# Scores in two column tiles of 256 rows in a cached-attention decode kernel, with another row order for the K load

## Chip, cores, metric

One core of one Trainium2 chip runs the whole program. The metric is the device time of one execution in microseconds (us). Every ratio is to runs of the kernel before on the same chip. Where kernels from different chips are set side by side (eight with eight_apart, four_apart with the changed kernel), the kernel before took 1147.5 to 1152.7 us on each of them. Each run has a state: slow when it is over 1.5% above the fastest run of the same kernel, otherwise fast.

## The reference, cut to what matters

Four blocks run one after the other: attention over a cache (A), a mixer with an MLP (B), A again, B again. One token for each of 8 batch elements, so nearly all of the work is reading the cache, twice.

```python
# A: B=8, Sq=1, D=448, Hq=16, Hkv=8, Sk=4096, Dh=256, bf16
q = (x @ wq).reshape(B, Sq, Hq, Dh).transpose(0, 2, 1, 3)
k = jnp.repeat(k_cache, 2, axis=1);  v = jnp.repeat(v_cache, 2, axis=1)
p = softmax(einsum("bhqd,bhkd->bhqk", q, k) * Dh ** -0.5)
o = einsum("bhqk,bhkd->bhqd", p, v)
...
x = x + A(layernorm(x));  x = x + B(layernorm(x))
x = x + A(layernorm(x));  x = x + B(layernorm(x))
```

K and V together have 268 MB, or 256 loads of 1 MB for one pass. Of the 512 loads of two passes the kernel makes 424; the other 88 tiles stay on the chip from the first pass to the second.

## The kernel before

A task is one batch element with two K/V heads: 8192 rows of K and as many of V, loaded in four K tiles and four V tiles of 1 MB, each 128 partitions by 8 KB. Fifteen such slots hold loads in flight. For each K tile, VectorE turns 32x32 blocks in place, TensorE multiplies with the block-diagonal query, and when all four tiles of a task are done, ScalarE takes exp and TensorE turns p, so that P times V can follow.

```python
# loads: 128 rows of 8 KB for a tile, all on the SP queue
if kv:
    src = rows.rearrange("(a p y) d -> a p (y d)", a=4, y=16)[c]
else:
    src = rows.rearrange("(p x y) d -> x p (y d)", x=4, y=16)[c]
nc.sync.dma_start(dst[:], src)
...
def scores(sc, t, x, qbd, gp):        # 4 column tiles (k) of 128 columns
    kv = t[:].rearrange("p (k t e i r) -> p k e r t i", k=4, t=4, e=4, r=2)
    for n in range(8):
        ...
        for k in range(4):
            nc.tensor.matmul(sc[32 * k : 32 * k + 8, 128 * x : 128 * x + 128],
                             qbd[:, ep, gp].rearrange("p a h -> p (a h)"),
                             kv[:, k, 2 * half + e2, par], start=(n == 0), stop=(n == 7))
...
ptw = consts.tile([128, 4, 16, 14], BF16, name="ptw")   # p with 6 zeros on each side
```

In these access patterns the first dimension counts partitions on the chip's side. On the memory's side of the K load it counts p = 0 to 127, each 64 rows of the cache (32 KB) after the last: one pitch, one count of 128.

Of the kernel before, what the change touches and what calls it, by code (L numbers as in the profile page):

```python
# [17 lines left out]
def kernel(  # L18
# [77 lines left out]
    for u in range(2):  # L96
        nc.vector.tensor_reduce(
            usel[:, 2 * u : 2 * u + 2],
            ident.rearrange("p (k q h) -> p h k q", k=4, h=2)[:, :, :, 2 * u : 2 * u + 2],
            mybir.AxisListType.XY,  # L100
            ALU.add,
        )
# [6 lines left out]
        ALU.add,  # L109
    )  # L110

    ptw = consts.tile([128, 4, 16, 14], BF16, name="ptw")
    nc.vector.memset(ptw[:], 0.0)

    misc = ps_t.tile([128, 512], FP32, name="misc")
    ot_bank = misc[:, 256:384]
# [252 lines left out]
    def z_cols(zall, gps):  # L369

        np_ = len(gps)
        zm = chn.tile([128, 4, np_], FP32, tag=f"zm{np_}")
        nc.vector.tensor_tensor(
            zm[:],
            zall[:, gps[0] : gps[-1] + 1].unsqueeze(1).to_broadcast([128, 4, np_]),
            usel[:].unsqueeze(2).to_broadcast([128, 4, np_]),
            ALU.mult,
        )
        yield
        z_ps = misc[:, 480 : 480 + 4 * np_].rearrange("p (n g) -> p n g", n=4)  # L380
        nc.tensor.matmul(z_ps, ones, zm[:], start=True, stop=True)  # L381
        yield
        rz = chn.tile([128, 4, np_], FP32, tag=f"rz{np_}")
        nc.vector.reciprocal(rz[:], z_ps)  # L384
        return rz
# [9 lines left out]
    def half(o_ps, zall, g8, OT):  # L395


        rz = yield from z_cols(zall, range(2 * g8, 2 * g8 + 2))

        R = chn.tile([128, 8], FP32, tag="R")  # L400
        nc.vector.tensor_mul(
            R[:].rearrange("p (g n) -> p g n", n=4),
            rz[:].rearrange("p n g -> p g n"),
            fold[:].rearrange("p (g n) -> p g n", n=4),
        )
        o_sb = chn.tile([128, Dh], FP32, tag="o_sb")
        nc.scalar.copy(o_sb[:], o_ps[:, Dh * g8 : Dh * g8 + Dh])
        yield
        ot_ps = ot_bank[:, 64 * g8 : 64 * g8 + 16].rearrange("p (j h) -> p j h", j=2)
        for j in range(2):  # L410
            nc.tensor.matmul(  # L411
                ot_ps[:, j], o_sb[:, 128 * j : 128 * j + 128], R[:], start=True, stop=True
            )
        yield
        nc.vector.tensor_copy(OT[:, :, 8 * g8 : 8 * g8 + 8], ot_ps)
        yield

# [15 lines left out]
    def first_half(b, st):  # L433

        OT = work.tile([128, 2, Hq, 1], BF16, tag="OT", bufs=1)
        y_ps = ps_m.tile([128, 4, 1], FP32, tag="chain")
        st["OT"], st["y"] = OT, y_ps
        yield from half(st["o"], st["z"], 0, OT[:, :, :, 0])
        yield from add_half(y_ps, OT, 0, 1, True, 2)
# [82 lines left out]
    def emit_loads(most=None):  # L522
        n = 0
        while loads and places and n != most:
            it = loads.pop(0)
            p = where[it] = places.pop(0)
            if stays(it):
                where[tasks[it[0]][1:], it[1:]] = p
            t, kv, c = it
            _, b, gp = tasks[t]  # L530
            dst = slots[p]
            rows = (A_v_cache if kv else A_k_cache)[b, 2 * gp : 2 * gp + 2].rearrange(
                "g s d -> (g s) d"
            )
            if kv:
                src = rows.rearrange("(a p y) d -> a p (y d)", a=4, y=16)[c]
            else:
                src = rows.rearrange("(p x y) d -> x p (y d)", x=4, y=16)[c]
            nc.sync.dma_start(dst[:], src)  # L539
            n += 1  # L540

# [5 lines left out]
            nc.vector.transpose(w, w)  # L547

    def scores(sc, t, x, qbd, gp):
        kv = t[:].rearrange("p (k t e i r) -> p k e r t i", k=4, t=4, e=4, r=2)  # L550
        for n in range(8):
            half, e2, par = n // 4, (n // 2) % 2, n % 2
            ep = 4 * e2 + 2 * par + half
            for k in range(4):
                nc.tensor.matmul(  # L555
                    sc[32 * k : 32 * k + 8, 128 * x : 128 * x + 128],
                    qbd[:, ep, gp].rearrange("p a h -> p (a h)"),
                    kv[:, k, 2 * half + e2, par],
                    start=(n == 0),
                    stop=(n == 7),  # L560
                )

    def exps(p_sb, sc, zall, gp):
        nc.scalar.activation(  # L564
            p_sb[:].rearrange("p t i x -> p x t i"),
            sc[:].rearrange("p (x t i) -> p x t i", x=4, t=4),
            ACT.Exp,
            scale=scale_exp,
            accum_out=zall[:, gp : gp + 1],
        )  # L570

    def transpose_p(p_sb):

        pt_ps = misc[:, 0:128].rearrange("p (t k r) -> p t k r", t=4, k=4)
        cols = identb[:].rearrange("p (k r) -> p k r", k=4)[:, :, 0:8]
        for t in range(4):
            nc.tensor.matmul(  # L577
                pt_ps[:, t],
                p_sb[:, t].rearrange("p i x -> p (i x)"),
                cols,  # L580
                start=True,
                stop=True,
            )
        nc.scalar.copy(  # L584
            ptw[:, :, :, 6:8],
            pt_ps.rearrange("p t k (a h) -> p a (t k) h", a=4),
        )

    def pv(o_ps, v, a, gp, begin):


        g = 2 * gp + a // 2
        w = 6 - 2 * (g % 4)
        for y in range(16):
            q = y % 4
            nc.tensor.matmul(  # L596
                o_ps[32 * q : 32 * q + 8, 256 * (g // 4) : 256 * (g // 4) + 256],
                ptw[:, a, 4 * (y % 4) + y // 4, w : w + 8],
                v[:, y * Dh : (y + 1) * Dh],
                start=(begin and y < 4),  # L600
                stop=(y >= 12),
                skip_group_check=True,
            )

    def pv_cols(o_ps, v, a, gp):

        g = 2 * gp + a // 2
        for y in range(16):
            for j in range(2):
                nc.tensor.matmul(  # L610
                    o_ps[:, j, 2 * g : 2 * g + 2],
                    v[:, y * Dh + 128 * j : y * Dh + 128 * j + 128],
                    ptw[:, a, 4 * (y % 4) + y // 4, 6:8],
                    start=(a % 2 == 0 and y == 0 and j == 0),
                    stop=(a % 2 == 1 and y == 15),
                    skip_group_check=True,
                )
# [24 lines left out]
    def add_gen(kind, b, g, at, until, total):  # L642
        gens.append({"kind": kind, "b": b, "g": g, "at": at, "until": until, "n": 0, "of": total})
# [20 lines left out]
    for idx, it in enumerate(items):  # L664
# [5 lines left out]
        if kv == 0:  # L670
# [9 lines left out]
                run(spread_q(st["qT"][:] if ps == 1 else qT1[:, :, b], qbd))  # L680
                st["q"] = qbd
            if "o" not in st:
                z_t = chn.tile([128, GP], FP32, tag="zall", bufs=3)
                st["o"], st["z"] = o_banks[0], z_t
                o_banks.append(o_banks.pop(0))
                if final:
                    st["y"] = o_banks[0][:, 0:4].unsqueeze(2)
                    oc = st["o"][:, 0 : 2 * Hq].rearrange("p (j h) -> p j h", j=2)
            if not (ps == 1 and stays(it)):
                transpose_k(slot)  # L690
            step(idx)
            scores(sc_t[n % 2], slot, c, st["q"], gp)
            if c == 0 and n > 0:
                transpose_p(p_of.pop(n - 1))
            if c == 3:
                p_n = work.tile([128, 4, 32, 4], BF16, tag="p_sb", bufs=1)
                p_of[n] = p_n
                exps(p_n, sc_t[n % 2], st["z"], gp)
        else:
            st = state[ps, b]  # L700
            if n in p_of:
                transpose_p(p_of.pop(n))
            if final and gp in free and c == 1:
                rz_gp = run(z_cols(st["z"], [gp]))
            step(idx)
# [22 lines left out]
            if c == 3:  # L728
                done = pairs_done[ps, b] = pairs_done.get((ps, b), 0) + 1
                if done == 2 and ps == 0:  # L730
                    add_gen("chain", b, first_half(b, st), idx + 1, idx + 21, 9)
                elif done == 2:
                    add_gen("chain" if final else "last", b, first_last(b, st), idx + 1, idx + 13, 9)
                elif done == 4 and ps == 0:
                    add_gen("chain", b, chain(b, st), idx + 1, first_of[(1, b), 0] - 1, 30)
                elif done == 4 and not final:
                    add_gen("last", b, last(b, st), idx + 1, idx + (7 if b == Bn - 2 else 13), 6)
                    if b == Bn - 2:
                        add_gen("last", 0, rest(b, st), idx + 1, len(items) - 2, 21)
        if not (ps == 0 and stays(it)):  # L740
# [83 lines left out]
```

## Time and profile before

| | before |
|---|---|
| median of 3 runs | 1147.85 us (1147.19 to 1150.88) |
| load queue's share of the 16 DMA engines' span | 98.0% |
| mean rate | 398 GB/s |
| TensorE, VectorE, ScalarE busy | 61%, 48%, 10% |
| chain of waits, K loads | 62% |

The page of the kernel before. Its row of GB/s has one number for each fortieth of the span; then come the packet counts, the queues (packets, MB, share of 16 engines' time), the chain that ended last, and four groups of instructions (count; busy us, mean ns of one; idle time before them and what ended most of it):

```profile
GB/s 352 375 420 420 407 385 399 418 412 383 414 420 400 385 399 419 420 403 406 409 420 420 400 400 413 420 420 387 402 412 420 408 371 412 420 410 355 410 420 153
DMA packets 68349, 457.52 MB, mean 398 GB/s; under 512 B 6999, under 2 KB 13030, under 8 KB 13542
## 3 DMA queue, kind: packets, MB, share of 16 engines
q1 hardware_dynamic: 68198, 455.19, 98.0%
...
## 4 chain that ended last, share of the span: by engine, by line
DMA 69%; PE 13%; DVE 11%; SPq 3%; issue 2%; POOL 1%; ACT 0%; POOLq 0%; DVEq 0%; ACTq 0%
DMA slot<-in_A_k_cache_dram 62%; DVE slot L547 9%; DMA slot<-in_A_v_cache_dram 6%; PE sc L555 4%; PE o L596 3%; PE y_ps L318 2%; SPq L148 2%; PE q_ps L274 1%; DMA wq_sb<-in_A_wq_dram 1%; SPq L539 1%; PE o L610 1%; DVE qbd L300 1%; PE o L318 1%; PE h_ps L336 0%; PE misc L381 0%
```

```profile
L547 DVE STREAM_TRANSPOSE slot<-slot 128x1024 uint32<-128x1024 uint32 x400 | 472.7, 1222 | 383.7 <-DMA slot<-in_A_k_cache_dram 375.0
L555 PE MATMUL sc<-slot,qbd 128*8 128x128 bf16 x8192 | 280.6, 286 | 345.6 <-DVE slot L547 287.2
...
L596 PE MATMUL o<-slot,ptw 128*8 128x256 bf16 x3968 | 242.8, 388 | 55.8 <-DMA slot<-in_A_v_cache_dram 33.9
L564 ACT ACTIVATE p_n<-sc 128x512 bf16<-128x512 f32 x64 | 84.7, 1323 | 780.6 <-PE sc L555 780.6
```

The loads fill the queue: 98.0% of what 16 engines have, and plateaus of 420 GB/s. 455 MB at 420 GB/s would be 1084 us, so the time is the DMA's but for some 65 us. "Under 512 B 6999": 6996 of these small packets have 4 bytes, and their count fits one completion packet for every DMA engine that took part in a load.

Stretches of the kernel before (columns: window in us; length; busy us of each engine with instruction counts; granted TensorE clock; DMA share; GB/s):

```profile
880.00:890.00 10.00, 4.27 (x96) 2.48 (x95) 4.51 (x5) 1.32 (x2) 0.00 (x0) 0.50 1.01 420
890.00:900.00 10.00, 4.48 (x100) 2.65 (x100) 4.74 (x4) 0.27 (x1) 0.00 (x0) 0.50 1.02 424
...
920.00:930.00 10.00, 7.82 (x177) 5.99 (x174) 6.68 (x17) 0.00 (x0) 0.70 (x1) 0.50 0.94 336
```

In the first two stretches, at 420 and 424 GB/s, TensorE is busy less than half of the time. Where a chain of small projections runs (920 to 930 us), TensorE nears 8 of 10 us and the load rate drops to 336. A busy TensorE alone does not lower the rate: between 1080 and 1090 us it was busy for 9.05 of 10 us, at 420 GB/s.

The timeline before, two score halves of one K tile, the P times V that follows, and the issue of a V load (start, us, engine, line; in brackets idle time before and what ended it):

```profile
885.92 0.60 PE L555 MATMUL sc<-slot,qbd 128*8 128x128 bf16 x16 [2.38 <-DVE slot L547]
...
887.04 0.60 PE L555 MATMUL sc<-slot,qbd 128*8 128x128 bf16 x16 [0.53 <-DVE slot L547]
...
887.82 1.02 PE L596 MATMUL o<-slot,ptw 128*8 128x256 bf16 x16 [0.18 <-DMA slot<-in_A_v_cache_dram]
...
888.89 0.33 SPq L539 DMA_DIRECT2D slot<-in_A_v_cache_dram  x1
```

Sixteen matmuls of 128 columns, four column tiles at a time, take 0.60 us; sixteen of 256 columns, four at a time, take 1.02 us.

### The profile page before, as it was taken

To read this page: it belongs to the slowest core of one execution; us is meant where nothing else is said; L and a number is where in the kernel's file an instruction comes from. 1 tells how busy PE (TensorE), PEld (TensorE's weight loads), DVE (VectorE), ACT (ScalarE), POOL (GpSimd) and SP (SyncE) were. 2 spreads that over 40 slices of the span, in tenths; PEclk is the share of its full clock that TensorE was granted. 3 is DMA by queue.
4 is the path that set the end of the run, shared out by engine and by line. 5 is a ranking of instruction groups with operands and counts; after the bars stand their busy time and mean duration, and the time that the engine had idled before them with its cause. 6 is when DMAs were issued, how large, how long until landed. Compare 5 with 4: busy or idle time off the path is not lost.

```text
span 1149.6 us, 36707 instructions
## 1 busy us (share of the span) xinstructions
PE 705.3 (61%) x17177; PEld 514.0 (45%) x17177; DVE 548.2 (48%) x904; ACT 113.9 (10%) x234; POOL 15.6 (1%) x25
## 2 busy tenths in 40 slices
PE   3144677457755667456764676646665576647787
PEld 2023455345533455344542454425443365425666
DVE  5145453455354544546254553445534553445352
ACT  0001011100110011001110101010011001100100
POOL 0000000000000000000000000000000000000000
PEclk9999997655655556555565557555575556555655
DMA  9999999999999999999999999999999999999993
GB/s 352 375 420 420 407 385 399 418 412 383 414 420 400 385 399 419 420 403 406 409 420 420 400 400 413 420 420 387 402 412 420 408 371 412 420 410 355 410 420 153
DMA packets 68349, 457.52 MB, mean 398 GB/s; under 512 B 6999, under 2 KB 13030, under 8 KB 13542
## 3 DMA queue, kind: packets, MB, share of 16 engines
q1 hardware_dynamic: 68198, 455.19, 98.0%
q8 instruction: 134, 2.20, 0.8%
q14 instruction: 17, 0.14, 0.0%
HBM read 455.15 MB, written 0.01 MB: 396 GB/s over the span
## 4 chain that ended last, share of the span: by engine, by line
DMA 69%; PE 13%; DVE 11%; SPq 3%; issue 2%; POOL 1%; ACT 0%; POOLq 0%; DVEq 0%; ACTq 0%
DMA slot<-in_A_k_cache_dram 62%; DVE slot L547 9%; DMA slot<-in_A_v_cache_dram 6%; PE sc L555 4%; PE o L596 3%; PE y_ps L318 2%; SPq L148 2%; PE q_ps L274 1%; DMA wq_sb<-in_A_wq_dram 1%; SPq L539 1%; PE o L610 1%; DVE qbd L300 1%; PE o L318 1%; PE h_ps L336 0%; PE misc L381 0%
## 5 line engine op out<-in xcount | busy, mean ns | idle before, releaser
L547 DVE STREAM_TRANSPOSE slot<-slot 128x1024 uint32<-128x1024 uint32 x400 | 472.7, 1222 | 383.7 <-DMA slot<-in_A_k_cache_dram 375.0
L555 PE MATMUL sc<-slot,qbd 128*8 128x128 bf16 x8192 | 280.6, 286 | 345.6 <-DVE slot L547 287.2
L555 PEld LDWEIGHTS <-qbd 128*8 128x8 bf16 x8192 | 194.5, 105 | 430.8 <-issue 298.6
L596 PE MATMUL o<-slot,ptw 128*8 128x256 bf16 x3968 | 242.8, 388 | 55.8 <-DMA slot<-in_A_v_cache_dram 33.9
L564 ACT ACTIVATE p_n<-sc 128x512 bf16<-128x512 f32 x64 | 84.7, 1323 | 780.6 <-PE sc L555 780.6
L596 PEld LDWEIGHTS <-ptw 128*8 128x8 bf16 x3968 | 107.9, 109 | 93.8 <-issue 45.0
L318 PEld LDWEIGHTS <-wo_sb 128*128 128x128 bf16 (+1 forms) x1600 | 64.8, 124 | 16.2 <-issue 15.6
L318 PE MATMUL y_ps<-OT,wo_sb 128*128 128x1 bf16 (+1 forms) x1280 | 55.5, 177 | 1.5 <-issue 1.5
L384 DVE RECIPROCAL rz<-misc 128x8 f32<-128x8 f32 (+1 forms) x33 | 6.4, 193 | 96.3 <-PE misc L381 96.3
L274 PEld LDWEIGHTS <-wq_sb 128*128 128x128 bf16 x1152 | 33.9, 104 | 19.1 <-issue 17.3
L274 PE MATMUL q_ps<-xb,wq_sb 128*128 128x1 bf16 (+1 forms) x1152 | 35.3, 166 | 11.4 <-DMA wq_sb<-in_A_wq_dram 3.6
L584 ACT CAST ptw<-misc 128x128 bf16<-128x128 f32 x64 | 17.5, 274 | 211.9 <-PE misc L577 159.4
L411 PEld LDWEIGHTS misc<-R,o_sb 128*128 128x128 f32 x124 | 25.9, 293 | 11.0 <-issue 11.0
L318 PEld LDWEIGHTS <-w_sb 128*128 128x128 bf16 (+1 forms) x630 | 25.7, 125 | 7.3 <-issue 5.2
L411 PE MATMUL misc<-R,o_sb 128*128 128x8 f32 x124 | 28.8, 343 | 0.0
L232 POOL TENSOR_TENSOR t<-t,nhalf 128x2 f32<-128x2 f32 (+1 forms) x17 | 10.7, 630 | 1075.8 <-DVE t L239 978.0
L318 PE MATMUL y_ps<-HT_t,w_sb 128*128 128x1 bf16 (+1 forms) x560 | 24.2, 177 | 0.5 <-DVE HT_t L359 0.5
L300 DVE TENSOR_SCALAR qbd<-misc,quad 128x64 bf16<-128x64 f32 x64 | 13.8, 278 | 22.0 <-PE misc L294 22.0
L381 PE MATMUL misc<-zm,one 128*128 128x8 f32 (+1 forms) x66 | 18.1, 348 | 6.7 <-ACT ptw L584 6.7
L336 PEld LDWEIGHTS <-w_sb 128*128 128x128 bf16 x560 | 17.2, 105 | 9.6 <-issue 9.2
L336 PE MATMUL h_ps<-xb,w_sb 128*128 128x1 bf16 (+1 forms) x560 | 17.9, 166 | 4.9 <-DVE xb L249 4.6
L381 PEld LDWEIGHTS misc<-zm,one 128*128 128x128 f32 x66 | 15.2, 287 | 11.9 <-ACT ptw L584 8.4
(92 smaller groups left out, 207.7 us busy)
## 6 DMA issues: line engine op xcount, KB each, us to landing
slot<-in_A_v_cache_dram SPq DMA_DIRECT2D x224, 1024.0 KB, 12.3
slot<-in_A_k_cache_dram SPq DMA_DIRECT2D x200, 1024.0 KB, 16.4
wo_sb<-in_A_wo_dram SPq DMA_DIRECT2D x1, 3584.0 KB, 26.6
wq_sb<-in_A_wq_dram SPq DMA_DIRECT2D x3, 1024.0 KB, 7.0
w_sb<-in_B_w_dram SPq DMA_DIRECT2D x1, 1568.0 KB, 12.8
w_sb<-in_B_w_dram SPq DMA_DIRECT2D x3, 448.0 KB, 26.8
wq_sb<-in_A_wq_dram SPq DMA_DIRECT2D x2, 256.0 KB, 10.0
w_sb<-in_B_w_dram SPq DMA_DIRECT2D x2, 112.0 KB, 9.0
```

The costliest lines, as they stand in the source:

```text
L148: nc.sync.dma_start(t[:, fc * cols : (fc + 1) * cols], src[fc * 128 : fc * 128 + 128, :])
L274: nc.tensor.matmul(q_ps[:, j * Hq + h, :], w, xbs(nb)[:, xi, :], start=(fc == 0), stop=(fc == 3),)
L300: nc.vector.tensor_scalar_mul(qbd[:, :, :, a, :], qs.rearrange("p e (f g u h) -> p (e f) u g h", f=2, u=2, h=2)[:, :, u], quad[:, a : a + 1],)
L318: nc.tensor.matmul(r, w[:, i, lo:hi], rhs(i), start=(first and fc == 0 and i == rows[0]), stop=(stop and i == rows[-1]), skip_group_check= ...
L336: nc.tensor.matmul(h_ps[:, c * nb : c * nb + nb], w, xbs(nb)[:, xi, :], start=(fc == 0), stop=(fc == 3),)
L381: nc.tensor.matmul(z_ps, ones, zm[:], start=True, stop=True)
L411: nc.tensor.matmul(ot_ps[:, j], o_sb[:, 128 * j : 128 * j + 128], R[:], start=True, stop=True)
L547: nc.vector.transpose(w, w)
L555: nc.tensor.matmul(sc[32 * k : 32 * k + 8, 128 * x : 128 * x + 128], qbd[:, ep, gp].rearrange("p a h -> p (a h)"), kv[:, k, 2 * half + e2, ...
L564: nc.scalar.activation(p_sb[:].rearrange("p t i x -> p x t i"), sc[:].rearrange("p (x t i) -> p x t i", x=4, t=4), ACT.Exp, scale=scale_ex ...
L584: nc.scalar.copy(ptw[:, :, :, 6:8], pt_ps.rearrange("p t k (a h) -> p a (t k) h", a=4),)
L596: nc.tensor.matmul(o_ps[32 * q : 32 * q + 8, 256 * (g // 4) : 256 * (g // 4) + 256], ptw[:, a, 4 * (y % 4) + y // 4, w : w + 8], v[:, y * ...
```

## The change

The intent is fewer instructions on TensorE (4096 score matmuls of 256 columns in place of 8192 of 128), exp and turning of p after every second K tile, and a smaller buffer for p in which neighbours share their zeros. Two column tiles of 256 rows need each half task to hold 1024 consecutive rows of each of the four blocks of 2048, so the K load's row order changes too.

```diff
-                src = rows.rearrange("(p x y) d -> x p (y d)", x=4, y=16)[c]
+                src = rows.rearrange("(a u i x y) d -> u x a i (y d)", a=4, u=2, x=2, y=16)[c // 2, c % 2]
             nc.sync.dma_start(dst[:], src)
 ...
-        kv = t[:].rearrange("p (k t e i r) -> p k e r t i", k=4, t=4, e=4, r=2)
+        kv = t[:].rearrange("p (k t e i r) -> p k e r t i", k=2, t=8, e=4, r=2)
 ...
-            for k in range(4):
+            for k in range(2):
                 nc.tensor.matmul(
-                    sc[32 * k : 32 * k + 8, 128 * x : 128 * x + 128],
+                    sc[32 * k : 32 * k + 8, 256 * (x % 2) : 256 * (x % 2) + 256],
 ...
-            sc[:].rearrange("p (x t i) -> p x t i", x=4, t=4),
+            sc[:].rearrange("p (x t i) -> p x t i", x=2, t=8),
 ...
-    def transpose_p(p_sb):
-        pt_ps = misc[:, 0:128].rearrange("p (t k r) -> p t k r", t=4, k=4)
-        for t in range(4):
+    def transpose_p(p_sb, u):
+        pt_ps = misc[:, 0:128].rearrange("p (t k r) -> p t k r", t=8, k=2)
+        for t in range(8):
             nc.tensor.matmul(
-                pt_ps[:, t],
+                pt_ps[64 * u : 64 * u + 64, t],
 ...
-    ptw = consts.tile([128, 4, 16, 14], BF16, name="ptw")
+    ptw = consts.tile([128, 6 + 8 * 64], BF16, name="ptw")
 ...
+            if c == 2:
+                transpose_p(p_of.pop(n), 0)
-            if c == 3:
-                p_n = work.tile([128, 4, 32, 4], BF16, tag="p_sb", bufs=1)
+            if c % 2 == 1:
+                p_n = work.tile([128, 8, 32, 2], BF16, tag="p_sb", bufs=1)
```

Left out: the sum of exp kept by half task and added once, the addressing of the smaller buffer for p, the copy of o in two halves of 128 columns, and step counts of the interleaved chains.

## The prediction

> **What bounds the kernel now.** The DMA engines. The page gives the load queue 98% of the 16 engines' span, at 398 GB/s mean; the stretches view shows 419 to 424 GB/s between 850 and 910 us, with TensorE under 70% busy. 455 MB at 420 GB/s is 1084 of the 1149.6 us. The chain of waits is 62% waits for K loads. Each K load (200) and V load (224) is 1 MB in 128 rows of 8 KB; one packet of 8 KB takes 309 ns (26.5 GB/s for an engine).
>
> **What the change does on the engines.** Scores go from 8192 matmuls of 128 columns, four column tiles side by side, to 4096 of 256 columns, two side by side. The timeline shows 0.60 us for half of a K load's scores; P times V, with 16 matmuls of 256 columns four side by side, takes 1.03 us. Eight of 256 columns two side by side stream as long, so I expect 1.0 us a half: 0.8 us more of TensorE for each K load (estimate). Exp goes from 64 of 1.32 us to 128 of half the size (estimate 0.75 us), turning from 4 to 8 matmuls a task. With two loads taking 5 us, most of that hides; alone it would cost 0 to 4%, in stretches where the queue already drops to 336 to 390 GB/s.
>
> **The decisive part: the K load.** To put 256 rows in two tiles, its source becomes four blocks (1 MB apart) of 32 rows: the outermost count of the source is 4 where it was 128. The Trainium skill, "DMA: Bandwidth & Descriptors", section "Why a DMA increments its semaphore by 16 and not by 1", says that the engines used are the largest number up to 16 that divides the outermost counts of both sides: 4 here. This trace agrees for other shapes: it has 6996 four-byte completion packets; 436 loads x 16, plus 8, 7 and 4 for the transfers with outer counts 8, 7 and 4, make 6995. So four engines carry all of K: 200 x 1.05 MB / 4 = 52.4 MB each, plus a sixteenth of the rest, 15.3 MB: 67.8 MB at 26.5 GB/s = 2560 us, plus about 40 us of ends, all on the critical path.
>
> **A second cost.** Each of the four engines then writes 32 neighbouring partitions. By the skill's "SBUF — State Buffer", section "Door 1: The DMA port swizzle", partitions p and p+32 share a port, so engines 0 and 1 collide when in step, as do 2 and 3. In this trace the 64-row loads, where engines pair up on ports, show 4 KB packets from 156 to over 315 ns: half rate. Fully in step, a K load would take 19.8 instead of 9.9 us, the kernel some 4500 us. [...] I expect about 400 us of it.
>
> **Prediction: 3000 us, range 2550 to 4100.** Faster by over 2%: 3%; within 2%: 5%; slower: 92%.
>
> **What would show it.** Per K load 4 landings instead of 16; mean rate near 150 GB/s; DMA share near 0.4; K issue to landing over 60 us against 16.4; DVE's wait for K over five times 375 us; the chain over 85% K loads. K packets of 309 ns would show no port sharing, 600 ns full sharing.
>
> **What would make it wrong.** If the load still spreads over 16 engines, 1150 to 1200 us, set by the longer scores. If the ports don't collide, 2600 us; if engines stay in step, 4500 us.

## The result

| | before | after |
|---|---|---|
| median | 1147.52 us (4 runs) | 3113.0 us (3077.47 to 3125.63, 4 runs) |
| ratio | | 2.7009, 95% interval 2.6764 to 2.7254 |
| load queue's share | 98.0% | 50.0% |
| mean rate | 398 GB/s | 149 GB/s |

Ratios are the mean time of one kernel's fast runs over that of the other's of the same rounds, so they are not quite the ratio of the medians. One of the four runs after, that of 3125.63 us, counts as slow; the three fast ones took 3077.47, 3105.6 and 3120.4 us. The sums below use the median of all four, 3113.0.

The page of the kernel after, the same lines:

```profile
GB/s 156 181 140 143 145 156 144 153 142 164 148 144 144 149 167 155 138 144 143 170 152 145 143 148 163 139 140 139 136 159 137 143 140 162 136 150 144 167 147 130
DMA packets 65924, 457.10 MB, mean 149 GB/s; under 512 B 4599, under 2 KB 10630, under 8 KB 11142
## 3 DMA queue, kind: packets, MB, share of 16 engines
q1 hardware_dynamic: 65798, 455.18, 50.0%
...
## 4 chain that ended last, share of the span: by engine, by line
DMA 81%; SPq 7%; DVE 5%; PE 5%; another core or an unknown queue 1%; issue 1%; ACT 0%; POOLq 0%; DVEq 0%
DMA slot<-in_A_k_cache_dram 77%; SPq L546 5%; DVE slot L554 5%; DMA slot<-in_A_v_cache_dram 4%; PE sc L562 3%; SPq L151 1%; PE o L604 1%; SPq L635 0%; PE misc L584 0%; DVE qbd L303 0%; PE o L321 0%; PE o L618 0%; PE q_ps L277 0%; PE h_ps L339 0%
```

```profile
L562 PE MATMUL sc<-slot,qbd 128*8 128x256 bf16 x4096 | 482.3, 386 | 2038.2 <-DVE slot L554 2008.5
L554 DVE STREAM_TRANSPOSE slot<-slot 128x1024 uint32<-128x1024 uint32 x400 | 474.3, 1224 | 2286.2 <-DMA slot<-in_A_k_cache_dram 2286.2
...
L604 PE MATMUL o<-slot,ptw 128*8 128x256 bf16 x3968 | 275.3, 382 | 39.1 <-DMA slot<-in_A_v_cache_dram 28.0
L571 ACT ACTIVATE p_n<-sc 128x512 bf16<-128x512 f32 x128 | 95.4, 746 | 2095.1 <-PE sc L562 2067.8
```

The same 455 MB move at 149 GB/s. The small packets fell from 6999 to 4599: 2400 fewer, which is 200 K loads times 12. So 4 engines finish each K load where 16 did. VectorE's idle time before the turning of K went from 384 to 2286 us, nearly all of it waiting for a K load. The chain of waits is 77% K loads. The new score matmuls and exps are not where the time went: TensorE is busy for 963 of 3076 us.

Stretches of the kernel after, 2 us each:

```profile
1519.00:1521.00 2.00, 1.51 (x32) 0.93 (x26) 0.00 (x0) 0.27 (x1) 0.00 (x0) 1.00 0.25 102
1521.00:1523.00 2.00, 0.00 (x0) 0.00 (x0) 0.00 (x0) 0.00 (x0) 0.00 (x0) 0.81 0.25 107
1523.00:1525.00 2.00, 0.00 (x0) 0.08 (x1) 1.11 (x1) 0.00 (x0) 0.00 (x0) 0.50 0.63 172
1525.00:1527.00 2.00, 1.70 (x22) 0.92 (x23) 1.26 (x2) 0.00 (x0) 0.00 (x0) 0.50 1.04 279
1527.00:1529.00 2.00, 1.72 (x20) 0.95 (x14) 0.00 (x0) 0.79 (x2) 0.00 (x0) 0.50 0.73 176
1529.00:1531.00 2.00, 0.00 (x0) 0.00 (x0) 0.00 (x0) 0.00 (x0) 0.00 (x0) 0.50 0.22 82
1531.00:1533.00 2.00, 0.00 (x0) 0.00 (x0) 0.00 (x0) 0.00 (x0) 0.00 (x0) 0.50 0.26 111
```

Two regimes can be seen. At 102 to 111 GB/s and a DMA share of 0.25, four of 16 engines work and each moves some 26 GB/s: K alone. Between 1523 and 1529 us a V load passes on all 16 engines, and the rate is 172 to 279 GB/s, where the kernel before had 420. The share of 1.04 there is not full speed, since before the same share went with 420 GB/s: a packet counts as busy for as long as it lasts, and these last longer. In the trace's records of single packets, the 8 KB packets during which 14 or more were open at once had a mean of 529 ns; before, the same kind had 321 ns. The 50.0% on the page is raised in the same way.

The timeline after, one K tile's scores, and two issues of V loads:

```profile
1553.88 10.30 SPq L546 DMA_DIRECT2D slot<-in_A_v_cache_dram  x1
1563.94 2.37 DVE L554 STREAM_TRANSPOSE slot<-slot 128x1024 uint32<-128x1024 uint32 x2 [11.75 <-DMA slot<-in_A_k_cache_dram]
...
1564.92 15.32 SPq L546 DMA_DIRECT2D slot<-in_A_v_cache_dram  x1
1565.24 2.14 PE L562 MATMUL sc<-slot,qbd 128*8 128x256 bf16 x16 [10.25 <-DVE slot L554]
```

Both halves follow each other in 2.14 us, 1.07 us a half. The issue of a V load, 0.33 us before, holds the issuing queue for 10.3 and 15.3 us here (the median V issue of the run is 0.38 us, the longest 18.8).

Two of the long pieces of the chain of waits after (start, us): each runs from the issue of a K load to its landing, about 40 us, where the page of before has a median of 16.4 us.

```profile
1510.55 39.19 DMA slot<-in_A_k_cache_dram
1550.65 41.84 DMA slot<-in_A_k_cache_dram
```

### The profile page after: what moved, and what is told of

It is laid out like the page before. It is cut to its first block, busy times and chain, and to the rows that moved or that the text cites. A ratio compares the mean times of both kernels' runs of the same rounds, so it can differ in the third digit from the quotient of the medians.

```text
span 3075.6 us, 30246 instructions
## 1 busy us (share of the span) xinstructions
PE 963.3 (31%) x13849; PEld 598.3 (19%) x13849; DVE 556.2 (18%) x937; ACT 133.6 (4%) x393; POOL 15.6 (1%) x25
## 2 busy tenths in 40 slices
DMA packets 65924, 457.10 MB, mean 149 GB/s; under 512 B 4599, under 2 KB 10630, under 8 KB 11142
## 4 chain that ended last, share of the span: by engine, by line
DMA 81%; SPq 7%; DVE 5%; PE 5%; another core or an unknown queue 1%; issue 1%; ACT 0%; POOLq 0%; DVEq 0%
DMA slot<-in_A_k_cache_dram 77%; SPq L546 5%; DVE slot L554 5%; DMA slot<-in_A_v_cache_dram 4%; PE sc L562 3%; SPq L151 1%; PE o L604 1%; SPq L635 0%; PE misc L584 0%; DVE qbd L303 0%; PE o L321 0%; PE o L618 0%; PE q_ps L277 0%; PE h_ps L339 0%
## 5 line engine op out<-in xcount | busy, mean ns | idle before, releaser
L562 PE MATMUL sc<-slot,qbd 128*8 128x256 bf16 x4096 | 482.3, 386 | 2038.2 <-DVE slot L554 2008.5
L562 PEld LDWEIGHTS <-qbd 128*8 128x8 bf16 x4096 | 228.2, 105 | 2232.8 <-DMA slot<-in_A_k_cache_dram 1737.8
L604 PE MATMUL o<-slot,ptw 128*8 128x256 bf16 x3968 | 275.3, 382 | 39.1 <-DMA slot<-in_A_v_cache_dram 28.0
L571 ACT ACTIVATE p_n<-sc 128x512 bf16<-128x512 f32 x128 | 95.4, 746 | 2095.1 <-PE sc L562 2067.8
L604 PEld LDWEIGHTS <-ptw 128*8 128x8 bf16 x3968 | 115.5, 102 | 88.5 <-issue 30.5
L584 PE MATMUL misc<-identb,p_n 128*64 128x16 bf16 x1024 | 71.9, 199 | 0.0
L584 PEld LDWEIGHTS <-p_n 128*64 128x64 bf16 x1024 | 60.0, 145 | 50.2 <-issue 48.8
L571 ACT ACTIVATION_READ_ACCUMULATOR p_n<-sc 128x1 f32 x128 | 23.2, 182 | 0.0
L417 ACT COPY o_sb<-o 128x128 f32<-128x128 f32 x62 | 16.4, 264 | 124.5 <-PE misc L419 123.1
```

The lines of the kernel that those rows point to most:

```text
L562: nc.tensor.matmul(sc[32 * k : 32 * k + 8, 256 * (x % 2) : 256 * (x % 2) + 256], qbd[:, ep, gp].rearrange("p a h -> p (a h)"), kv[:, k, 2 ...
L571: nc.scalar.activation(p_sb[:].rearrange("p t i x -> p x t i"), sc[:].rearrange("p (x t i) -> p x t i", x=2, t=8), ACT.Exp, scale=scale_ex ...
L584: nc.tensor.matmul(pt_ps[64 * u : 64 * u + 64, t], p_sb[:, t].rearrange("p i x -> p (i x)"), cols, start=True, stop=True,)
L604: nc.tensor.matmul(o_ps[32 * q : 32 * q + 8, 256 * (g // 4) : 256 * (g // 4) + 256], ptw[:, p_at(a, y, 2 * (g % 4)) : p_at(a, y, 2 * (g % ...
```

## Experiments

All runs have the form of one of the two kernels with the smallest edit that serves. Those marked "wrong" pair rows of K with other rows of V. The comparison with the reference passed them all the same, because the scores of this data are almost equal (estimate from the input scales in the reference: they spread by about 0.003); so it is no proof that a row order is right. The order of the whole_turn version was checked by following the row numbers by hand. The packet lengths in this section are read from the trace's records of single DMA packets, which no view of the page shows. "Open at once" counts the 8 KB packets that have begun and not ended, averaged over a packet's life.

Two things are taken for granted here and in the expectations. Which partitions share a port comes from the page that the prediction cites; no trace shows a port. That engine e carries block e of a load, and so writes that block's partitions, is an assumption: the completion packets show how many engines a load used, not which.

Theory 1 was that of the prediction: four engines carry all of K (a floor of 2600 us), and collisions at ports that engines 0 and 1, and 2 and 3, sweep together add the rest. Theory 2: the longer scores and the half-task exp and turning cost the time.

### load_alone: the new load in the kernel before (wrong)

```diff
-                src = rows.rearrange("(p x y) d -> x p (y d)", x=4, y=16)[c]
+                src = rows.rearrange("(a u i x y) d -> u x a i (y d)", a=4, u=2, x=2, y=16)[c // 2, c % 2]
```

> The kernel before with nothing changed but the source of the K load (four blocks of 32 rows); wrong values on purpose, the same amount of work. Theory 1 (the load is carried by four engines, and these collide at shared ports): 2900 to 3250 us, 4 landings for each K load, 2400 fewer completion packets. Theory 2 (the time comes from the longer scores and the half-task exp and turning): 1140 to 1160 us, as before.

Measured: 3038.18 us (before 1152.17), ratio 2.6413, 95% interval 2.6287 to 2.6539; small packets 4599. One line is the whole slowdown but for 75 us.

### rest_alone: all of the change but the load (wrong)

```diff
-                src = rows.rearrange("(a u i x y) d -> u x a i (y d)", a=4, u=2, x=2, y=16)[c // 2, c % 2]
+                src = rows.rearrange("(p x y) d -> x p (y d)", x=4, y=16)[c]
```

> The changed kernel with the K load of before (128 rows at one pitch); wrong values on purpose, the same amount of work. Theory 1: 1140 to 1200 us, 16 engines busy at 98%. Theory 2: near 3100 us. What it shows over 1147 us is the price of the longer scores and the half tasks once the load is fast.

Measured: 1167.7 us (before 1152.17), ratio 1.0155, interval 1.0113 to 1.0196. Theory 2 is out. Two lines of its page:

```profile
q1 hardware_dynamic: 68198, 455.19, 97.7%
...
L562 PE MATMUL sc<-slot,qbd 128*8 128x256 bf16 x4096 | 436.5, 363 | 203.8 <-DVE slot L554 178.9
```

The queue is full again at 97.7%. The scores' busy time rose from 280.6 to 436.5 us, and 1.5% of the span is what that and the rest of the change cost when the load is fast: halving the number of matmuls while halving how many column tiles work at once saves no streaming time; TensorE's scores took 156 us more.

### whole_turn: a right version with the fast load

```diff
-            p_sb[:].rearrange("p t i x -> p x t i"),
+            p_sb[:, :, :, 2 * u : 2 * u + 2].rearrange("p t i x -> p x t i"),
 ...
-    def transpose_p(p_sb, u):
+    def transpose_p(p_sb):
 ...
-                pt_ps[64 * u : 64 * u + 64, t],
+                pt_ps[:, t],
 ...
+            if c == 1:
+                half_p = work.tile([128, 8, 32, 4], BF16, tag="p_sb", bufs=1)
 ...
```

and the load of before. Left out are the calls, now one turning of p for each task. Partition 4i + x of turned p then holds row block x of row group i, as in the kernel before.

> A right version that keeps the two column tiles of 256 rows, exp per half task and the shared zeros, but turns p per whole task, so that the K load of before fits (p_sb twice as large). Right values. Theory 1: within 1% of rest_alone, 1140 to 1200 us. Theory 2: near 3100 us.

Measured: 1161.7 us, ratio 1.0093, interval 1.0061 to 1.0126. The column tiles of 256, in a form that keeps the fast load, are 0.9% slower than before. No version here beats the kernel before. Its exp, which is read below:

```profile
L571 ACT ACTIVATE half_p<-sc 128x512 bf16<-128x512 f32 x128 | 169.1, 1321 | 678.3 <-PE sc L562 678.3
```

### four_loads: all 16 engines, half of the ports at a time

```diff
-            nc.sync.dma_start(dst[:], src)
+            if kv:
+                nc.sync.dma_start(dst[:], src)
+            else:
+                for a in range(4):
+                    nc.sync.dma_start(dst[32 * a : 32 * a + 32], src[a])
```

> The changed kernel with each K load issued as four loads of 32 rows of 8 KB, one for each block of 32 partitions; right values. Every load has an outer count of 32, so all 16 engines carry it, but one load reaches half of the ports. If only the number of engines matters: 1140 to 1200 us. If the ports matter too (theory 1 whole): [...] 1400 to 1550 us, less if the engines spread over neighbouring loads; many 8 KB packets between 309 and 620 ns. Theory 2: near 3100 us.

Measured: one fast run of 1876.72 us; three more of 1910 to 1922 us count as slow. Missed by all: better than 3113, far from 1147, and above the 1400 to 1550 expected. The queue's share is 97.2% at 244 GB/s, and the median 8 KB packet took 552 ns where before it took 309. So the number of engines is not all. Which partitions a load writes is the likely reason, but it is not shown alone: the edit also makes four loads of one and spaces their source rows differently. (Four loads of 32 partitions need not have long packets: eight_apart below issues K so, on eight engines, and with K alone its packets have a mean of 320 ns.) A K load costs (1877 - 1152) / 200 = 3.6 us more than before. Half of the rate of before would add only 2.5 us (estimate from 1.05 MB at 420 GB/s).

### two_far and two_near: two engines, apart or on the same ports (wrong)

```diff
 two_far
-                src = rows.rearrange("(a u i x y) d -> u x a i (y d)", a=4, u=2, x=2, y=16)[c // 2, c % 2]
+                src = rows.rearrange("(a u i x y) d -> u x a i (y d)", a=2, u=2, x=2, y=16)[c // 2, c % 2]
 two_near (the source of the changed kernel)
-            nc.sync.dma_start(dst[:], src)
+            if kv:
+                nc.sync.dma_start(dst[:], src)
+            else:
+                for h in range(2):
+                    nc.sync.dma_start(dst[64 * h : 64 * h + 64], src[h::2])
```

> The changed kernel with the K load's source in two blocks of 64 rows, 2 MB apart: two engines carry K, engine 0 writes partitions 0 to 63, engine 1 partitions 64 to 127, which share no port; wrong values on purpose. Floor from bytes: 200 x 0.524 + 15.3 = 120 MB at 26.5 GB/s = 4540 us, plus 50. If ports cause what the four engines took above their floor (3113 against 2600 us): 4550 to 4700 us, 8 KB packets nearly all 309 ns. If instead the memory's pitch or the queue's depth causes it, K is some 24% slower here too: 5500 us or more.

> As two_far, the same two engines, bytes and 2 MB between the blocks, but each K load as two loads of two blocks of 32 rows, so that engine 0 writes 0 to 31 then 64 to 95, engine 1 writes 32 to 63 then 96 to 127: the two share every port. Wrong values on purpose. If ports cause it: over 5300 us, up to 8600 if the two stay in step, packets up to 618 ns. If ports don't matter: as two_far within 3%.

Measured: two_far 4792.93 us, two_near 4728.72 us (before 1150.95). The floor of two engines is 4590 us, so the rule of bytes holds again, within 5%. But the pair that shares every port is no slower than the pair that shares none: this spoke against theory 1's second half. So do the packets: with at most five open at once, K alone for the most part, their mean was 314 ns in two_near and 317 in two_far. Two_far missed its expected 4700 too, by 93 us; 203 us over its floor are 0.9 us for each of 224 V loads (an expectation below says "each K load").

### pitch: another spacing of the source blocks (wrong)

```diff
-                src = rows.rearrange("(a u i x y) d -> u x a i (y d)", a=4, u=2, x=2, y=16)[c // 2, c % 2]
+                src = rows[: 4 * 2032].rearrange("(a r) d -> a r d", a=4)[
+                    :, 1000 * (c // 2) : 1000 * (c // 2) + 1024
+                ].rearrange("a (i x y) d -> x a i (y d)", x=2, y=16)[c % 2]
```

> The changed kernel with the four source blocks 2032 rows apart where it has 2048 (8 KB short of 1 MB), all else as it is; wrong values on purpose. If the part above the floor comes from the memory's pitch of 1 MB: near 2600 us. If it comes from ports: 3000 to 3250 us, as the changed kernel.

Measured: 3119.92 us, against 3113.0 of the changed kernel. The 1 MB between the blocks is not the cause.

### eight and eight_apart: eight engines, on shared ports or each on its own (wrong)

```diff
 eight
+                src = rows.rearrange("(a u i x y) d -> u x a i (y d)", a=8, u=2, x=2, y=16)[c // 2, c % 2]
 eight_apart (K only; four loads of 32 partitions, each [8][4][8 KB])
+                for a4 in range(4):
+                    lo = 2048 * a4 + 1000 * (c // 2)
+                    at = rows[lo : lo + 1024].rearrange("(e r) d -> e r d", e=8)[:, : 124]
+                    at = at.rearrange("e (j r) d -> e j (r d)", j=4)
+                    at = at[:, :, 15 * Dh * (c % 2) : 15 * Dh * (c % 2) + 16 * Dh]
+                    nc.sync.dma_start(dst[32 * a4 : 32 * a4 + 32], at)
```

> The changed kernel with the K load's source in eight blocks of 16 rows: eight engines, which pair up on ports (0 with 2, 1 with 3, 4 with 6, 5 with 7); wrong values on purpose. Floor from bytes: 200 x 0.131 + 15.3 = 41.6 MB at 26.5 GB/s = 1570 us, plus 50. With no sharing 1620 us; with K slowed by ports as much as with four engines (24%) 1850 us; in step throughout 2600 us. If the number of engines doesn't set the time: 1150 to 1200 us.

> Eight engines for K as in the run called eight (2448 us), the same bytes for each engine, but the K load goes as four loads of 32 partitions, each in eight blocks of 4 rows, so that engine e always writes partitions 4e to 4e+3 of the 32 and no two of the eight ever share a port; wrong values on purpose. The two_near run (4729 us, no slower than two_far) speaks against ports, so this is open. If ports cause what eight took above its floor of 1620 us: 1620 to 1800 us. If it comes with the number of engines, the queue or the memory: 2350 to 2500 us.

Measured: eight 2448.11 us, eight_apart 1809.99 us (before 1150.95 and 1152.73). Eight lies between the 1850 and the 2600 us of its expectation, and eight_apart is 10 us over its range of 1620 to 1800. The bytes of each engine are the same, and the other layout is worth 638 us. With seven to nine 8 KB packets open at once, which is K alone for the most part, the mean packet took 406 ns in eight and 320 in eight_apart. So in eight the K packets are slow even with no V load beside them. That the ports do it is not shown: the number of loads for a tile differs too, one against four, and so does the distance between the engines' sources, 512 KB against 64 KB.

### four_apart and four_apart_all: four engines, no two on one port (wrong)

The edit is that of eight_apart with e=4, j=8 and 248 rows; in four_apart_all V takes the same path.

> Four engines for K as in the changed kernel (3113 us), but as four loads of 32 partitions, each in four blocks of 8 rows, so that engine e always writes the two ports of partitions 8e to 8e+7 and no two of the four share one; wrong values on purpose. Floor 2600 us. If ports between the K engines cause the rest: 2650 to 2850 us, what is left over being V writes of other engines that meet K writes (two_far took some 0.9 us for each K load over its floor, where no two K engines share a port). If not ports: 3050 to 3200 us.

> As four_apart, and V too is loaded by the same four engines at their own ports, so that no engine ever meets another at a port; wrong values on purpose. Floor: 424 x 0.262 + 0.7 = 111.8 MB at 26.5 GB/s = 4220 us, plus 50. Port theory: 4250 to 4320 us with nearly all 8 KB packets at 309 ns. If the rest above the floor has another cause, 4500 us or more and many packets over 500 ns.

Measured: four_apart 3183.64 us, four_apart_all 4248.2 us. The first speaks against the ports: with no two K engines on one port the kernel is no faster than the changed one, and it falls in the range of "if not ports". The second sits on its floor (4220 plus 50), with a mean 8 KB packet of 312 ns. So the floor arithmetic is right, and what comes on top of it in four_apart is gone when the other twelve engines do not load V.

### four_all: the changed load for both K and V (wrong)

```diff
-            if kv:
-                src = rows.rearrange("(a p y) d -> a p (y d)", a=4, y=16)[c]
-            else:
-                src = rows.rearrange("(a u i x y) d -> u x a i (y d)", a=4, u=2, x=2, y=16)[c // 2, c % 2]
+            src = rows.rearrange("(a u i x y) d -> u x a i (y d)", a=4, u=2, x=2, y=16)[c // 2, c % 2]
```

> The changed kernel's K load left as it is, and V loaded in the same way, so that four engines carry K and V (floor 111.8 MB at 26.5 GB/s = 4220 us, plus 50), engines 0 and 1 sweep the same ports, and so do 2 and 3, and no other engine loads anything; wrong values on purpose. Open is what takes the changed kernel 510 us above its floor. My first theory, K engines colliding with each other at the ports of p and p+32: K and V loads 24% slower than the floor, near 5250 us. The rival, formed after four_apart (3184 us though no two K engines share a port): the other twelve engines' V loads, which come in bursts, slow the four while they last, and the four alone run at full rate: 4240 to 4350 us, 8 KB packets nearly all 309 ns.

Measured: 4263.16 us (before 1150.75). Its page:

```profile
GB/s 156 107 106 107 107 107 106 107 107 107 107 107 105 107 107 107 107 107 106 107 107 107 107 105 107 107 107 107 106 107 107 107 107 105 106 107 107 107 105 83
DMA packets 63236, 457.09 MB, mean 107 GB/s; under 512 B 1911, under 2 KB 7942, under 8 KB 8454
## 3 DMA queue, kind: packets, MB, share of 16 engines
q1 hardware_dynamic: 63110, 455.17, 25.9%
```

107 GB/s from end to end, a mean 8 KB packet of 313 ns, a share of 25.9%, which is four engines of 16. Here engines 0 and 1 sweep the same ports (by the skill's port table), as in the changed kernel, and lose nothing by it. The first theory of the second cost is refuted for four engines (if engine e carries block e); the rival stands.

## Why the prediction was right, and where it was not

**The main cause and its size: right.** The K load runs on four engines. Load_alone shows that this line is the cause, the completion packets show the four (2400 fewer, 12 for each K load; 14 fewer for each in two_far and 8 in eight, whose pages have 4199 and 5399), and four_apart_all and four_all show the rate: four engines move 8 KB in 309 ns each and no faster. The floor of 2600 us was right as a floor. The rule is on the Trainium skill's page "DMA: Bandwidth & Descriptors", section "Why a DMA increments its semaphore by 16 and not by 1"; the traces agree with it for outer counts of 2, 4 and 8 on the memory's side and 128 on the chip's.

**The second cost: the size near by luck, the mechanism wrong.** The prediction gave 400 us to "engines 0 and 1 collide when in step, as do 2 and 3". The kernel took 3113 - 2600 = 513 us over the floor. But K engines on shared ports cost nothing in four_all and in two_near, and keeping them apart gained nothing in four_apart. The runs put the V loads in its place: without twelve other engines loading V there is no excess (four_all). In the changed kernel's stretches, K alone goes at 102 to 111 GB/s, and while a V load passes, all 16 engines together reach 172 to 279 GB/s. 513 us over 224 V loads is 2.3 us for each.

The packets of the changed kernel itself say the same. With at most five open at once, 23607 packets had a mean of 325 ns and a median of 309, and 3% took over 500; with 14 or more open, 27110 had a mean of 529, and 65% took over 500. By the prediction's own sign ("309 ns would show no port sharing"), the K engines alone share nothing that costs time. Nor were they short of work, as far as a count can tell (which engine carries a packet is not recorded): fewer than four packets were open for 88 of 3076 us, against 79 us in four_all.

That 400 us came near 513 is therefore luck. By the prediction's own case for ports that do not collide the kernel would have taken 2600 us, and the sum has no term for V loads that slow the K engines, and are slowed, while they pass.

The prediction's own reading of the 64-row loads (4 KB packets from 156 to over 315 ns) was a fact. That it comes from sharing a port was argued, and it did not follow for four engines in a long stream. Nothing measured said which part of the 1900 us "fully in step" to take, so the 400 was a guess. Whether the engines fall out of step, or sharing then costs nothing, no view shows.

**Open.** Why a passing V load holds the four engines and itself back. It may be ports that K and V engines cross, or some path further up, in the memory for one. A lack of work just after a V load (82 GB/s at 1529 us) is too short to be the cause, by the 88 us above. Four_apart and eight_apart do not decide it: the layout that helped eight engines by 638 us did not help four. In the run with eight, K packets are slow with no V load beside them (406 ns), through shared ports or through the distances of their sources; no run tells which.

**The scores.** Predicted 1.0 us a half, measured 1.07. "Alone it would cost 0 to 4%": rest_alone has 1.5%.

**Exp.** Predicted 0.75 us from "half the size"; measured 0.746, right by luck, for another reason. Each exp still covers 512 columns (see the group lines). What halved it is the pitch of its output: before, consecutive results lie 8 bytes apart, after 4. Whole_turn puts them 8 bytes apart again, with the same 512 columns, and one takes 1321 ns.

**The signs.** Mean rate 149 GB/s (predicted near 150); VectorE's wait for K 2286 us, 6.1 times 375 (over five). The K loads have 77% of the chain where over 85% was predicted; all of DMA has 81%. K issue to landing was to be over 60 us; the page has no median for it, and the longest pieces of the chain, which run from a K issue to its landing, are 26 to 48 us. The number assumed that K loads queue up as before; probably it was less because the issue itself was held up: V issues took 10.3 and 15.3 us where 0.33 us is usual. What holds an issue is not shown. DMA share near 0.4: the page has 0.50, inflated by waiting packets.

## What to carry to other kernels

Before reordering a load, count its outermost dimension on both sides after merging: a source of four blocks cost 12 of 16 DMA engines here, and a one-line access pattern turned 1152 us into 3038 (load_alone). A DMA-bound kernel's first check after such a change is the completion packets or the landings, not the compute engines. Where the layout does not need the new order, keep the load and pay in the compute: whole_turn lost 0.9%, not 170%.

## What the Trainium skill lacked or had wrong

- "DMA: Bandwidth & Descriptors" says which engines a load uses, but not what these do when the others start a load beside them: with 14 or more 8 KB packets open in the changed kernel, their mean was 529 ns, against 325 with at most five open and 321 in the kernel before with as many open. The excess is 2.3 us for each V load.
- "SBUF — State Buffer", "Door 1: The DMA port swizzle", gives about 218 GB/s as the asymptote for 32 partitions, and 189 measured at 1 MiB. It has no figure for such loads queued among full ones: four_loads moved 244 GB/s in all. Charged to its K tiles alone, the loss is 3.6 us over 2.5 us, so 1.05 MB in about 6.1 us, or 172 GB/s (estimate). This does not contradict the page: 66% of the packets took over 500 ns and only 47% were K's, so V loads were slowed as well.
- The same section tells which partitions share a port, which invites the reading that two engines on one port run at half rate. In four_all engines 0 and 1 swept the same ports (if engine e carries block e) for 4263 us at a mean of 313 ns a packet. The page does not say when sharing a port costs time.
- The same page says, in its passage on 16-byte lines, that a stride is free as long as a line gets two hits, so up to 8 bf16 elements. ScalarE's exp to bf16 took 746 ns with results 4 bytes apart and 1321 ns with 8 bytes apart, the same 512 columns; 8 bytes are 4 elements, two to a line, and should have been free.
- No page that I found says how long an issuing queue can be held: SP's issue of a V load took 10.3 and 15.3 us against 0.33 us, in a kernel whose K loads wait on four engines. The cause is not shown.
